# Delta-rule attention and an MLP in one kernel: whole-array first units, blocked weights, and a new static order

## The chip, the cores and the metric

The kernel runs on one core of a Trainium2 chip. A core has five engines with queues of their own: TensorE (PE, matrix products, written to the PSUM banks), VectorE (DVE), ScalarE (ACT), GpSimd (POOL) and SyncE (SP, which mostly issues DMAs). The metric is the device time of one execution in microseconds (us); the runs of one kernel on one chip are summed up by their median.

## The reference

For 4 batches and 8 heads, a recurrence runs over 768 tokens with a 48 x 48 state per head, and the result, 3072 tokens of 384 numbers, goes through an MLP:

```
k_n = k / (norm(k) + 1e-6)
for t in range(768):
    y[t]  = q[t] @ state
    v_old = state.T @ k_n[t]
    state = state + beta[t] * outer(k_n[t], v[t] - v_old)
x = y, heads side by side          # 3072 x 384
h = x @ w_in                       # 384 x 2048
out = gelu_tanh(h) @ w_out         # 2048 x 384
```

Inputs and output are float32; inside, the kernel works in bfloat16 with float32 sums.

## The kernel before

**Chunks and units.** The 768 tokens are cut into 12 chunks of 64. Within a chunk the recurrence is solved with matrices: the 64 x 64 triangular system of the chunk is inverted, and one state is carried from chunk to chunk. A chunk has two units (two batches each, 8 heads, so 128 partitions hold two batches by 64 tokens): 24 units u, 12 chunks c. For each unit `prep(u)` normalises k (`kn`), multiplies by beta (`kb`), casts q (`qb`), transposes the three (`T` on TensorE into `kT`; from unit 10 on by a DMA), builds two Gram matrices (`G2`, `G`) that VectorE copies under triangular masks into `ln` and `wp`, and inverts the triangle in five rounds of a Newton-like iteration. A round has a product `A` on TensorE, an addition `rt` (in rounds 4 and 5 the narrower `rl`) on VectorE, a product `B` on TensorE and a copy of `B` out of PSUM to be the next round's left operand `xi`.

**Two forms of a product.** For units 2 and up the left operand stands block-diagonally in `bd` (two 64 x 64 blocks in a 128 x 128 matrix), so that a product is 8 matmuls of the whole array (`L577`); the copies of `B` go into `bd` in two halves on ScalarE or VectorE (`bde`), or by way of `xi` and GpSimd (`bdc`), and the first round's `bd` is written by two GpSimd selects (`X1`). For units 0 and 1 (`u < TILED`) the operand stays in `xi` as two 64 x 64 halves, and a product is 16 matmuls on quarters of the array (`L580`); one copy on ScalarE carries `B` into `xi`.

**State and MLP.** `chain(c)` then reads the state (`K`, `R`, `Q`), applies the inverse (`U`, copied to `us`), updates the state (`S`, `Sn`) and makes the output (`O`, copied to `xo`), which is transposed (`X`, `xT`). `mlp(c)` runs 48 up matmuls (3 to a block of 128 columns of w_in, `L715`), four gelu instructions on ScalarE (`L720`) and 32 down matmuls (`L728`), evicts two 128 x 384 results (`Z`) and stores them.

**What sets the order.** No engine's order is written by hand. Every operation is added to a list with its engine or engines, an estimated duration, what it reads and writes, and a key. `Flow.schedule` plays the list through on estimated times, takes at each engine the ready operation of the lowest key (with offsets from a table `KEYS` and some thresholds), and so fixes five queues; `Flow.emit` writes them out with semaphore waits. On the chip each queue then runs strictly in that order. For TensorE the planner counts instructions in blocks of 256 (`BLOCK`) and lets the next block come `REFILL` us after the last one was entered. `FILL` dummy matmuls on a zero tile `wz` (`L426`) are put in where the planner finds TensorE with nothing ready; what is left of them runs last.

**Weights.** `weights()` casts w_in and w_out to bfloat16 in DMAs that GpSimd issues: `W1` of [128, 3, 2048] and `W2` of [128, 16, 384], two DMAs each, so rows of 1024 and of 384 columns. They wait until k and q of chunks 1 and 2 have landed. GpSimd issues them in the midst of the preparation of units 2 to 5.

**Tables and norms.** `norms(c)` makes the reciprocal norms of k: a square, a reduce, a root (on ScalarE for the first three chunks), eps and a reciprocal.

Of the kernel before, what the change touches and what calls it, by code (L numbers as in the profile page):

```python
# [24 lines left out]
class Flow:  # L25
# [5 lines left out]
    SLACK = 3.316  # L31
    DMA_LAT = 2.6
    DMA_AHEAD = 4.0
    BLOCK, REFILL = 256, 4.2
    STALL_SLACK = 0.316
    YIELD = 0.524
    KEYS = {"A": (-7.71, -5.16), "B": (-8.97, -24.42), "G": (-2.84, -18.0), "G2": (-29.12, -32.55), "K": (-9.35, 7.5),
            "O": (-7.72, 20.33), "On": (-12.86, -26.48), "Q": (-2.61, 7.53), "R": (-5.21, 3.94), "S": (2.29, 5.4),
            "Sn": (1.11, -13.13), "T": (1.64, -15.61), "U": (-6.61, 14.58), "Un": (11.48, -26.2), "X": (-18.72, -0.83),
            "X1": (-10.44, 4.23), "Z": (-11.93, -59.74), "bdc": (-1.39, -1.66), "bde": (-0.39, -30.53), "bdz": (5.03, 48.53),  # L40
            "down": (14.54, 27.08), "eps": (6.96, -24.93), "gelu": (0.92, 27.76), "inv": (-28.92, 24.92), "kT": (12.35, -2.18),
            "kb": (-6.15, -0.06), "kn": (28.23, 13.15), "ladj": (-11.45, 74.91), "ln": (7.96, -17.35), "loadk": (3.9, -10.38),
            "loadq": (4.06, -4.84), "loadv": (5.61, -10.9), "out": (10.45, -36.55), "pow": (-0.57, 2.88), "qb": (4.0, 12.65),
            "rt": (-17.56, -11.96), "sq": (-16.33, 39.05), "sum": (29.93, -44.43), "tabG": (-22.77, 16.06),
            "tri": (16.56, -21.66), "turn": (0.89, -16.45), "turnx": (-22.16, -15.64), "up": (1.24, -3.93), "w1": (-6.75, 17.06),
            "w2": (30.51, 0.26), "wp": (7.96, -30.95), "xT": (-16.66, -39.38), "xi": (1.34, -6.31)}
    PEN = 8.000
    HOLD = 0.219
    SOON = 0.3
# [41 lines left out]
    def schedule(self):  # L91
# [22 lines left out]
        count, refilled = 0, 0.0  # L114
        self.stalled = 0.0
# [7 lines left out]

        def run_pe(o, t):
            d = o.dur + (self.SWITCH if o.mode != mode else 0.0)
# [4 lines left out]
            while n >= left:  # L130
# [5 lines left out]
                ref, left = x + self.REFILL, self.BLOCK  # L136
# [38 lines left out]
        while done < len(self.ops):  # L175
            for e in ENGINES:
                while free[e] <= t + 1e-9:
                    o = choose(e)
# [118 lines left out]
def bass_deltanet__then__act_gelu_tanh_kernel(  # L297
# [13 lines left out]
    NU = 2 * NC  # L311
    DIRECT = lambda u: (2, 3, 4, 5) if u < 8 else (2, 4)
    GROUPS = [[c] for c in range(NC)]
    FILL = 60
    TILED = 2
    TURN, TURNX = 10, 5

    F = Flow()
    A = F.add
# [475 lines left out]
```

## Time and profile before

| | |
|---|---|
| median of 3 runs | 282.13 us (281.83 to 283.87) |
| the profiled execution's own time | 285.42 us |
| its span, from the first to the last instruction | 283.7 us |
| TensorE busy | 264.1 us, 93% |
| VectorE, ScalarE, GpSimd busy | 67%, 63%, 52% |
| mean granted TensorE clock | 0.976 |
| first up matmul of the MLP, last down matmul ended | 50.75 us, 279.96 us |

How to read a profile: a row of a timeline has start, duration, engine, line and operation, what it writes and reads, shapes and count, and in brackets the idle time of the engine before it with what ended it. "issue" there means that the engine waited for nothing that the profile shows. PEld is TensorE's weight load, which overlaps the matmuls. Matmuls are pipelined, so that a row's duration holds some latency, and the distance from one start to the next is the time that it takes from the ones behind it. In the slices of the page the span is cut in 40 parts of 7.09 us; a digit is the busy share in tenths, and PEclk the granted clock in tenths of full speed. q1 is the queue of SyncE's DMAs, q0 that of GpSimd's, and q8 carries the engines' own code. Each run's time is a little longer than its span.

### The profile page before, as it was taken

Reading aid. Unit: us, or ns where it says so; the run is one execution under the profiler, and the core shown is the slowest. Engines: PE = TensorE matmul, PEld = TensorE weight load, DVE = VectorE, ACT = ScalarE, POOL = GpSimd, SP = SyncE. Lnnn points to the kernel's source line nnn. Section 1 sums busy time; section 2 is a strip of 40 time slices with the busy share of each in tenths; the row PEclk is TensorE's granted clock in tenths of the full one; section 3 lists DMA queues with packets and bytes.
Section 4 is the critical chain, followed back from the end, with each engine's and each line's share of the span. In section 5 each row is a group of like instructions: output and inputs, shape, how many; then the busy total and the mean of one; then the engine's idle time right before and its main releaser. Section 6 shows DMA issues by size and latency. Waiting matters only on the chain.

```text
span 283.7 us, 12884 instructions
## 1 busy us (share of the span) xinstructions
PE 264.1 (93%) x5849; PEld 201.6 (71%) x5860; DVE 189.0 (67%) x291; ACT 178.7 (63%) x274; POOL 147.3 (52%) x217
## 2 busy tenths in 40 slices
PE   4789487999999999899998999999999999999997
PEld 1356367787778777687777777778777787878663
DVE  7797556876977987787998857496576777430000
ACT  5715245699767775576785683786766775756421
POOL 4468810257899299787699895442443431200000
PEclk9999777799999999999999999999999999999999
DMA  7999999960698923999991392760696210300133
GB/s 122 164 163 175 196 187 161 156 110 2 125 154 144 166 36 65 159 174 160 173 124 31 70 145 45 146 111 2 116 140 116 58 30 5 58 2 2 30 83 83
DMA packets 109237, 29.72 MB, mean 105 GB/s; under 512 B 103296, under 2 KB 108416, under 8 KB 109184
## 3 DMA queue, kind: packets, MB, share of 16 engines
q1 hardware_dynamic: 104848, 25.47, 57.7%
q0 software_dynamic: 2880, 3.15, 7.0%
q8 instruction: 46, 0.75, 1.1%
q10 hardware_dynamic: 1456, 0.30, 0.5%
q14 instruction: 7, 0.06, 0.1%
HBM read 20.64 MB, written 4.72 MB: 89 GB/s over the span
## 4 chain that ended last, share of the span: by engine, by line
PE 83%; DVE 6%; ACT 5%; issue 4%; POOL 1%; POOLq 0%
PE ps L728 22%; PE ps L715 22%; PE ps L577 17%; PE ps L426 4%; PE ps L626 3%; PE ps L648 3%; PE ps L671 3%; PE ps L520 2%; ACT bd L369 2%; PE ps L580 2%; PE ps L536 2%; PE ps L544 2%; ACT gT L720 1%; PE ps L657 1%; DVE rt L587 1%
## 5 line engine op out<-in xcount | busy, mean ns | idle before, releaser
L715 PE MATMUL ps<-xT,W 128*128 128x256 bf16 x576 | 85.6, 274 | 0.6 <-ACT gT L720 0.3
L728 PE MATMUL ps<-W,gT 128*128 128x384 bf16 x384 | 74.5, 326 | 0.1
L369 ACT ACTIVATE bd<-ps 64x512 bf16<-64x512 f32 x93 | 54.8, 589 | 18.6 <-PE ps L577 17.2
L587 DVE TENSOR_TENSOR rt<-ps,two 128x512 bf16<-128x512 f32 x72 | 48.8, 686 | 17.6 <-PE ps L577 16.5
L720 ACT ACTIVATE gT<-ps 128x1024 bf16<-128x1024 f32 x48 | 48.8, 1022 | 15.6 <-PE ps L715 15.3
L369 ACT ACTIVATE xi<-ps 128x512 bf16<-128x512 f32 x57 | 33.6, 596 | 31.0 <-PE ps L577 17.7
L715 PEld LDWEIGHTS ps<-xT,W 128*128 128x128 bf16 x576 | 47.6, 98 | 7.7 <-ACT gT L720 0.8
L566 POOL TENSOR_SCALAR_AFFINE_SELECT bd<-ln 64x512 bf16<-64x512 bf16 x44 | 28.9, 656 | 41.2 <-DVE ln L548 37.6
L728 PEld LDWEIGHTS ps<-W,gT 128*128 128x128 bf16 x384 | 34.8, 98 | 17.8 <-issue 0.3
L570 POOL COPY bd<-xi 64x256 f32<-64x256 f32 x64 | 25.4, 397 | 32.5 <-ACT xi L369 24.9
L587 DVE TENSOR_TENSOR rl<-ps,two 128x384 bf16<-128x384 f32 (+1 forms) x48 | 23.1, 485 | 15.4 <-PE ps L577 12.2
L552 DVE CAST_PREDICATED wp<-mup,ps 128x1024 bf16<-128x1024 uint16 x24 | 29.2, 1218 | 2.4 <-PE ps L536 2.1
L488 POOL TENSOR_TENSOR nrm<-nrm,half 128x16 f32<-128x16 f32 x9 | 26.2, 2908 | 3.1 <-DVE nrm L485 2.7
L577 PE MATMUL ps<-wp,bd 128*128 128x64 bf16 (+1 forms) x528 | 25.6, 190 | 1.2 <-issue 0.8
L577 PE MATMUL ps<-rt,bd 128*128 128x64 bf16 x528 | 26.5, 195 | 0.2 <-DVE rt L587 0.2
L512 POOL TENSOR_TENSOR tok<-tok,bsb 128x384 bf16<-128x384 bf16 x23 | 18.7, 830 | 12.9 <-PE ps L657 6.4
L577 PEld LDWEIGHTS ps<-rt,bd 128*128 128x128 bf16 x528 | 22.6, 99 | 3.3 <-DVE rt L587 0.3
L577 PEld LDWEIGHTS ps<-wp,bd 128*128 128x128 bf16 x528 | 21.1, 99 | 4.6 <-issue 1.0
L369 ACT ACTIVATE ob<-ps 128x384 f32<-128x384 f32 x23 | 11.3, 490 | 16.0 <-PE ps L728 15.8
L426 PE MATMUL ps<-wz 128*128 128x512 bf16 x49 | 15.6, 445 | 5.0 <-POOL wz L375 4.0
L510 POOL TENSOR_TENSOR tok<-kraw,nrm 128x384 bf16<-128x384 f32 x22 | 17.9, 831 | 3.0 <-DVE nrm L492 2.8
L548 DVE CAST_PREDICATED ln<-mlo,ps 128x512 bf16<-128x512 uint16 x24 | 16.3, 684 | 4.6 <-PE ps L544 4.5
(90 smaller groups left out, 349.2 us busy)
## 6 DMA issues: line engine op xcount, KB each, us to landing
qraw<-in_q_dram SPq DMA_DIRECT2D x24, 192.0 KB, 5.3
vraw<-in_v_dram SPq DMA_DIRECT2D x24, 192.0 KB, 5.4
out_dram<-ob SPq DMA_DIRECT2D x48, 96.0 KB, 2.7
kraw<-in_k_dram SPq DMA_DIRECT2D x22, 192.0 KB, 5.3
W<-in_moe_w_in_dram POOLq DMA_DIRECT2D x2, 768.0 KB, 10.3
W<-in_moe_w_out_dram POOLq DMA_DIRECT2D x2, 768.0 KB, 13.4
kT<-tok SPq DMA_TRANSPOSE x14, 4.6
kraw<-in_k_dram ACTq DMA_DIRECT2D x2, 96.0 KB, 3.2
```

What stands on the lines that cost most here:

```text
L369: return e.activation(out, in_, ACT.Copy) if e is nc.scalar else e.tensor_copy(out, in_)
L426: ins = e.matmul(P(name)[:, :], wz[:, 0:128], wz[:, 0:512])
L488: e.tensor_tensor(nr[:, 1, hx], nr[:, 0, hx], half[:, hx], ALU.pow), {"act": 0.22, "pool": 1.65 * wd},
L512: A(POOL, z + "kb", lambda e, P: e.tensor_tensor(kb, kn, bcol, ALU.mult), tt, reads=[n("tok0"), *BS], writes=[n("tok1")], key=u)
L552: A("dve", z + "wp", lambda e, P: e.copy_predicated(wp[s][:, :, :], mup[:, :].bitcast(U16).unsqueeze(1).to_broadcast([128, H, 2 * C]), P(p ...
L566: A("pool", z + "X1", lambda e, P, src=src, dst=dst: e.affine_select(out=dst, in_=src, compare_op=ALU.not_equal, fill=1.0, base=0, pattern ...
L570: A("pool", z + "bdc", lambda e, P, src=src, dst=dst: e.tensor_copy(dst.bitcast(F32), src.bitcast(F32)), 0.42, reads=[n("xi")], writes=[w( ...
L577: ins = e.matmul(P(name)[:, C * h + lo:C * h + C], bd[m][:, h, :], rhs[:, h, lo:C])
L587: A("dve", z + "rt", lambda e, P, i=i, lo=lo, r_=r_: e.tensor_tensor(r_[:, :, lo:C], P(ps(f"A{i}")).rearrange("p (h t) -> p h t", h=H)[:, ...
L715: ins = e.matmul(P(ph)[:, w * f:w * f + w].rearrange("p (x t) -> p x t", x=2), W1[:, j, 128 * (i + f):128 * (i + f) + 128], x_[:, :, j, :] ...
L720: A("act", z + "gelu", lambda e, P, i=i, ph=ph: e.activation(g_[:, i:i + nf, 0:w], P(ph).rearrange("p (f t) -> p f t", f=nf), ACT.Gelu_app ...
L728: ins = e.matmul(P(po)[:, 0:DM], g_[:, f, 128 * b:128 * b + 128], W2[:, f, :], start=(f == 0), stop=(f == FC - 1))
```

## The change

Four things change together.

- **First units:** `TILED` is 0, so units 0 and 1 go the block-diagonal way too (8 whole-array matmuls to a product, selects on GpSimd for the first round, half copies after that).
- **Weights:** `W1` is kept as [128, 8, 3, 256] and `W2` as [128, 2, 16, 192]. Six DMAs fill `W1` and four `W2`, with rows of 256 and 192 columns. The up matmul's weights stay 128 columns side by side; the down matmul reads its 384 columns as two pieces of 192.
- **Engines:** the zero tile `wz` is written by VectorE first of all; q's cast for units 0 and 1 goes to ScalarE or VectorE instead of GpSimd or VectorE; one of the two first kT copies may go to ScalarE; the squares of chunks 1 and 2 go to ScalarE, and all norms of chunk 1 get a very early key.
- **Order:** the planner gets a TensorE clock (half speed after a window of 3.4 us that was not busy enough), a slower code refill while weights load, other thresholds and keys, and 110 dummies instead of 60. The first up of a chunk's MLP now also waits, in the plan, for the downs of three chunks earlier that read the same gelu buffer. All five queues come out in another order.

In the order for TensorE that results, 77 dummies stand ahead of the first up (48 before), 20 more between it and the last down (3 before) and 13 behind that (9 before); units 2 and 3 begin their rounds just ahead of the first up, where before they had done about half of them.

The core of the diff:

```diff
-    BLOCK, REFILL = 256, 4.2
+    BLOCK, REFILL = 256, 3.9
...
+    WINDOW = 3.413
+    PHASE = 1.094
+    SLOW = 2.4
+    LOW, HIGH = 0.6, 0.93
...
+        def roll(t):
+            nonlocal cold, edge, active
+            while edge <= t:
+                share = active / self.WINDOW
+                cold = share < (self.HIGH if cold else self.LOW)
+                edge, active = edge + self.WINDOW, 0.0
...
-            d = o.dur + (self.SWITCH if o.mode != mode else 0.0)
+            d = (o.dur + (self.SWITCH if o.mode != mode else 0.0)) * (2.0 if cold else 1.0)
...
-                ref, left = x + self.REFILL, self.BLOCK
+                ref, left = x + self.REFILL + (self.SLOW if crowd[0] < x < crowd[1] else 0.0), self.BLOCK
...
-    FILL = 60
-    TILED = 2
+    FILL = 110
+    TILED = 0
...
+    SQACT, EARLY, QBACT, KTACT = 3, -140, 1, 1
...
-        W1 = sb("W1", [128, J, FF])
-        W2 = sb("W2", [128, FC, DM])
+        W1 = sb("W1", [128, FC // 2, J, 256])
+        W2 = sb("W2", [128, 2, FC, DM // 2])
...
-            A("pool", "0wz", lambda e, P: e.memset(wz[:, :], 0.0), 0.5, writes=["wz"], key=-30)
+            A("dve", "1wz", lambda e, P: e.memset(wz[:, :], 0.0), 0.2, writes=["wz"], key=-200)
...
-            for i in range(2):
-                f0 = FF // 2 * i
-                A("pool", "w1", lambda e, P, f0=f0: e.dma_start(W1[:, :, f0:f0 + FF // 2], w1v[:, :, f0:f0 + FF // 2]), 4.7,
+            for i, j in [(i, j) for i in range(2) for j in range(J)]:
+                f0, b0 = FF // 2 * i, FC // 4 * i
+                A("pool", "w1", lambda e, P, j=j, f0=f0, b0=b0: e.dma_start(
+                    W1[:, b0:b0 + FC // 4, j, :], w1v[:, j, f0:f0 + FF // 2].rearrange("p (b f) -> p b f", f=256)), 4.7 / J, mm=0.35,
...
-            for i in range(2):
-                n0 = FC // 2 * i
-                A("pool", "w2", lambda e, P, n0=n0: e.dma_start(W2[:, n0:n0 + FC // 2, :], w2v[:, n0:n0 + FC // 2, :]), 4.7,
+            for i, y in [(i, y) for i in range(2) for y in range(2)]:
+                n0, e0 = FC // 2 * i, DM // 2 * y
+                A("pool", "w2", lambda e, P, n0=n0, y=y, e0=e0: e.dma_start(W2[:, y, n0:n0 + FC // 2, :], w2v[:, n0:n0 + FC // 2, e0:e0 + DM // 2]), 2.35, mm=0.5,
...
-                key = 2 * c + x
-                A("dve" if c == 0 else ("act", "pool"), z + "sq", lambda e, P, sqx=sqx, kk=kk: e.activation(sqx, kk, ACT.Square) if e is nc.scalar else
+                key = 2 * c + x if c != 1 or not EARLY else EARLY
+                z = z if c != 1 or not EARLY else "1"
+                A("dve" if c == 0 else "act" if c < SQACT else ("act", "pool"), z + "sq", lambda e, P, sqx=sqx, kk=kk: e.activation(sqx, kk, ACT.Square) if e is nc.scalar else
...
-            A(POOL, z + "qb", lambda e, P: e.tensor_copy(qb, qr), {"pool": 0.5, "dve": 0.4}, reads=[f"qraw{r}"], writes=[n("tok2")], key=u + 0.01)
+            A((("act", "dve") if QBACT else POOL) if u < 2 else "pool", z + "qb", lambda e, P: copy(e, qb, qr), {"pool": 0.5, "dve": 0.4, "act": 0.55}, reads=[f"qraw{r}"], writes=[n("tok2")], key=u + 0.01)
...
-                      **(dict(alloc=(ph, 2)) if f == 0 else dict(accum=[ph])))
+                      **(dict(alloc=(ph, 2), writes=[f"{gn}s{i}"]) if f == 0 else dict(accum=[ph])))
...
-                            ins = e.matmul(P(po)[:, 0:DM], g_[:, f, 128 * b:128 * b + 128], W2[:, f, :], start=(f == 0), stop=(f == FC - 1))
+                            ins = e.matmul(P(po)[:, 0:DM].rearrange("p (y e) -> p y e", y=2), g_[:, f, 128 * b:128 * b + 128], W2[:, :, f, :], start=(f == 0), stop=(f == FC - 1))
```

## The prediction, made before the changed kernel was run

> **What bounds the kernel now.** I read the page first, for the engine shares and the slices, then TensorE's timeline between 26 and 62 us, then the chain of work that ended last near the end, and last the groups by shape. From the page:
>
> ```profile
> PE 264.1 (93%) x5849; PEld 201.6 (71%) x5860; DVE 189.0 (67%) x291; ACT 178.7 (63%) x274; POOL 147.3 (52%) x217
> ...
> PE   4789487999999999899998999999999999999997
> ...
> PEclk9999777799999999999999999999999999999999
> ...
> q1 hardware_dynamic: 104848, 25.47, 57.7%
> q0 software_dynamic: 2880, 3.15, 7.0%
> q8 instruction: 46, 0.75, 1.1%
> ```
>
> TensorE is the bound from slice nine (57 us) on; only in the first eight slices does it idle or run at a reduced clock. So the case splits in a head, where latency rules, and a body, where every TensorE instruction counts. The head, in TensorE's timeline:
>
> ```profile
> 34.54 0.50 PE L580 MATMUL ps<-wp,xi 64*64 64x32 bf16 x11 [3.12 <-issue]
> ...
> 38.13 0.92 PE L648 MATMUL ps<-rs,xi 64*64 64x48 bf16 x27
> ...
> 41.25 0.59 PE L671 MATMUL ps<-us,wp 64*64 64x48 bf16 x27 [0.98 <-issue]
> ...
> 47.57 0.27 PE L626 MATMUL ps<-st,kT 48*64 48x48 bf16 x10 [1.37 <-issue]
> ...
> 50.75 0.82 PE L715 MATMUL ps<-xT,W 128*128 128x256 bf16 x3
> ```
>
> Three waits for "issue" stand inside runs of equal matmuls. Counted in the built program (two instructions to a matmul, one to a separate wait), they lie 257 and 255 instructions apart, and q8 moved 46 pieces of 16 KB for 11,825 instructions: TensorE waited for its own code, at 34.54, 41.25 and 47.57, so one block of 256 took 6.7 and 6.3 us to come while the weights were loading. Late in the run the next such waits end a block of 3.7 us (111.98 to 115.70). A rule of the Trainium skill (Runtime: NRT & Kernel Launch, Instruction fetch mechanics) is that crossing a block costs little and is mostly hidden; these three rows speak against it, and by it the sum below would be 2.5 us lower.
>
> The first MLP matmul starts at 50.75. From the chain near the end:
>
> ```profile
> 256.45 3.93 PE ps L715 x36
> ...
> 264.96 14.95 PE ps L728 x92
> ...
> 279.96 1.89 PE ps L426 x8
> ```
>
> An up matmul takes 3.93/36 = 0.109 us, a down 14.95/92 = 0.1625, and the last down ends at 279.96, 3.7 before the span's end (an eviction and a store).
>
> **TensorE's sum, part by part.** In the same way the chain and the timeline give 0.22 us for one block-diagonal product of 8 (three of them, x24, in 0.67), 0.37 for one of 16 quarter-array matmuls (20.36 to 20.73), 0.056 for a transpose, 0.216 for a dummy (1.89 for 8, with its latency), and 0.1 for each change between quarter-array and whole-array instructions (four downs behind such a change stand with 0.76 in the chain, else with 0.65). Multiplied with the order of instructions that each program gives TensorE:
> - Real work (all but dummies): before 239.9, after 233.4. Of the 6.5, 20 products of units 0 and 1 at 0.37 minus 0.23 give 2.9, and 194 changes of mode become 156, 38 by 0.1 = 3.7.
> - Before the first up: before 21.1, after 13.3, since units 2 and 3 no longer invert ahead of it. From there to the last down: before 218.8 and 3 dummies (0.65), after 220.1 and 20 dummies (4.3). The last 13 dummies (2.8) lie beside the final store (3.7) and cost nothing.
> - Against the trace: 279.96 - 50.75 = 229.2, so the body loses 9.8 that the sum does not hold: about 1.3 to the half clock until 53, 8.5 to short waits.
>
> W2 is now read in two pieces of 192 columns. The up matmul already reads its moving operand in two pieces of 128 and takes 0.109 us for 256 columns, so I add nothing.
>
> **The head.** The cast of q leaves VectorE for ScalarE (0.98), one kT copy too (0.91), but chunk 1's norms move between the masks of ln and wp: reduce 0.93, eps 0.4, reciprocal 0.25, and ln of unit 1 waits behind a reduce that waits for ScalarE's square. So wp of units 0 and 1 is done where it was, near 19.5, and the inversion starts as before (18.5). A round has four steps: product 0.42 until its consumer starts, rt 0.69, product 0.42, copy 0.6 to 0.69. VectorE bears two rt and two of the four half copies, 1.37 + 1.38 = 2.75, where ScalarE's xi copies left it 1.37 before. Two rounds at 2.8, one with the reduce (0.93) at 3.7, two with the shorter rl at 2.5 end at about 32.5; the xi copy, and U starts at 33.5. Before, U started at 38.13, 3.1 of that behind the code stall. That stall goes because a block-diagonal round issues half the matmuls; what is late next is again code: in the new order blocks end between O and S and just ahead of units 2 and 3's first products. With a block requested at 31.5 and 6.5 us each, TensorE gets them at 38 and 44.5. Without a stall, the copies of kT, us, two wp, two ln and the state on VectorE (0.95 + 0.96 + 2.4 + 1.4 + 0.95 ahead of kT of unit 4) let the first up start at 42. So 42 and 44.5 bound it.
>
> **Ten weight DMAs.** GpSimd's two rows are these:
>
> ```profile
> L471 POOL DMA_DIRECT2D W<-in_moe_w_out_dram x2 | 1.8, 911 | 0.0
> L467 POOL DMA_DIRECT2D W<-in_moe_w_in_dram x2 | 1.8, 878 | 0.0
> ```
>
> 1024 rows cost what 384 do, but both move the same bytes: an issue costs 0.9 per DMA, or in proportion to bytes 0.3 (w1, a third) and 0.45 (w2, half). Six w1 take 1.8 to 5.3 us against 1.75. Behind them on GpSimd stand the casts, kn and kb of units 2 and 3 (1.0, 1.65, 1.62), which start after the four selects (about 18.2): unit 2's tokens are ready at 23.8 to 27. TensorE's order holds unit 2's transpose ahead of unit 1's second product of round two, due at 23.9, so all behind it waits 0 to 3 us. The two rows cannot part the ends; I take the middle, 0.6, which makes 1.4 late, and 1 of it reaches the first up: 45.5. On cost by DMA the Trainium skill (DMA: Bandwidth & Descriptors, Anatomy of one DMA) says that many descriptors can be emitted before the added cost shows, and lists the fixed part apart; it speaks for the upper end, and with it the sum would be about 2 higher.
>
> Bytes on the queues: q1's packets of 243 B mean took 0.577 x 16 x 283.7 / 104848 = 25 ns, q0's of 1094 B 110 ns, in both 10 B per ns, so 512 and 384 B rows cost no more by byte. With twice the rows against q1's, and q1 served in between, I expect w2 to end near 50 where it ended near 44; the first downs are due past 52. That cover is 2 to 4 us.
>
> **Sum.** First up 45.5, work 220.1, dummies 4.3, short waits 8.5, half clock after the idle head 2.0 (as before, since TensorE does about 3.5 us of work between 34 and 44.5), tail 3.7: a span of 284.1. The profiled execution had a span of 283.7 and took 285.42, the runs' median is 282.13: 285.8 x 282.13/285.42 = **282.5 us, no change**. The first up comes 5 us sooner, and the work that stood ahead of it, with 17 more dummies, is paid behind it.
>
> **Rivals.**
> - Faster: the smaller packets let code through in the 3.7 us of the late blocks, and dummies keep the clock up. First up 42, no half clock: 278.6, which is **277.1 us**. For it: 77 dummies ahead of the first up, where the old order has 48. Against it: 2 KB packets (until 31) and 768 B packets (after) made code equally late.
> - Slower, decided by the price of one issue on GpSimd: from 0.6 up it holds unit 2's transpose, and with it TensorE's queue. At 0.9 the first up is at 47.5, span 286.1, **284.5 us**; with the weights later by the same 3 us and the first downs waiting on them up to 2 more, 286.5.
> - The body loses more: the new order's 20 dummies mark places where its plan found nothing ready, and if TensorE's short waits there rise by half again (8.5 to 13) and the second half of W2 is late by 1: 289.6, **288 us**. Against it: VectorE and ScalarE are busy 67% and 63%, and their work hardly changes.
> - It doesn't do what it says: the changes of mode cost nothing because they lie in waits. Then 3.7 come back, **286.2 us**; it counts with the third case.
>
> **How the numbers follow.** About 1% (2.8 us) is what a measurement of this kernel can tell from no change. Forecast 0.37, faster rival 0.28, slower rival 0.22 (half of it beyond 1%), body rival 0.13. Faster by over 1%: 0.28; within: 0.37 + 0.11 = 0.48; slower: 0.11 + 0.13 = 0.24. The range 277 to 288 leaves out the outer parts of the first and last rivals, some 0.15.
>
> **What would show it.** First up at 45 to 46 and waits for "issue" of 1 to 2.5 us at S and ahead of it; GpSimd's W issues between 0.3 and 0.9 us; unit 2's first transpose at 24 to 27; the clock under full between 36 and 49; VectorE's bd copies 8 before U. A first up at 42 or below, or a body with under 6 us of waits, makes it faster and this wrong; W2 landing after 54 makes it slower.

## The result and the profile after

The changed kernel takes **296.2 us** (median of 4 runs, 296.16 to 296.98) where the kernel before takes 282.95 (281.83 to 283.87): a ratio of **1.046** (95% interval 1.042 to 1.050). This ratio and those below leave out runs more than 1.5% above the fastest of their kernel. The forecast was 282.5, the range 277 to 288: it was wrong. The profiled execution of the changed kernel took 296.16 with a span of 294.3.

The page of the changed kernel, its lines that answer to those shown of before (busy time and instructions; the slices, now 7.36 us each; the DMA queues):

```profile
PE 273.6 (93%) x5750; PEld 204.1 (69%) x5750; DVE 196.2 (67%) x310; ACT 176.8 (60%) x269; POOL 145.6 (49%) x219
...
PE   8995955999899999899998999899999999999998
...
PEclk9997995999999999999999999999999999999999
...
q1 hardware_dynamic: 104848, 25.47, 54.8%
q0 software_dynamic: 7328, 3.15, 8.4%
q8 instruction: 45, 0.74, 1.1%
```

TensorE has 110 matmuls fewer (PEld has 5860 and 5750; the trace of before lacks 11 records of PE) and is busy 9.5 us longer: busy time also holds the dummies, 110 instead of 60, and the stretches at half clock. In the row of slices, from slice nine to the last but one, four stand below nine tenths, where before had two.

TensorE's timeline of the changed kernel around the head (start, duration, what it does, and in brackets the idle time ahead of it):

```profile
25.89 1.46 PE L545 MATMUL ps<-ident,tok 128*128 128x128 bf16 x12 [2.95 <-POOL tok L537]
...
36.55 0.62 PE L673 MATMUL ps<-rs,xi 64*64 64x48 bf16 x28
...
41.48 0.44 PE L682 MATMUL ps<-us,tok 64*64 64x48 bf16 x32 [2.50 <-DVE ln L573]
...
48.59 0.32 PE L561 MATMUL ps<-kT 48*64 48x128 bf16 x3 [2.76 <-issue]
...
49.69 2.11 PE L740 MATMUL ps<-xT,W 128*128 128x256 bf16 x9
```

Unit 2's transpose waits 2.95 us for GpSimd's tokens, U starts at 36.55, and two waits for code follow, at S and in the Gram matrices ahead of the first up. The one at 41.48 is put down to VectorE's `ln`; counted in the built program, it stands at instruction 194 of its block of 256, as the one at 48.59 (195) does, and in no_body_dummies below, whose queues are the same up to the first up, the wait there is put down to "issue". The block between them took 7.1 us. The first up starts at 49.69.

The end, from the chain of work that ended last:

```profile
283.35 7.15 PE ps L753 x44
290.50 2.81 PE ps L449 x13
```

The last down ends at 290.50 and the span 3.8 later, as before. So the time went here: first up 50.75 to 49.69 (1.1 sooner), first up to last down 229.2 to 240.8 (**11.6 longer**), the rest unchanged.

Where in the body? Windows of the two kernels (stretch, its length, busy time of PE with its instructions, then PEld, DVE, ACT, POOL, clock, DMA), before:

```profile
110.00:140.00 30.00, 29.20 (x805) 22.85 (x805) 24.43 (x38) 19.09 (x28) 23.98 (x37) 1.00 0.98 160
...
165.00:200.00 35.00, 34.45 (x858) 26.44 (x857) 24.01 (x35) 24.61 (x39) 17.77 (x33) 1.00 0.45 86
```

and after:

```profile
110.00:140.00 30.00, 27.56 (x758) 21.77 (x756) 24.57 (x39) 18.27 (x28) 22.62 (x34) 1.00 0.80 135
...
165.00:200.00 35.00, 32.67 (x801) 25.01 (x801) 28.70 (x43) 22.25 (x36) 18.62 (x37) 1.00 0.50 84
```

Over the body TensorE's idle time is 7.7 us (4.0 before), 3.1 of it in waits for code (1.4 before). At full clock it idles 2.4 and 2.3 us in these two stretches, where it idled 0.8 and 0.6, and part of its busy time there is dummies. One such place, in TensorE's timeline of the changed kernel:

```profile
187.72 0.36 PE L602 MATMUL ps<-wp,bd 128*128 128x32 bf16 x8
188.70 0.41 PE L602 MATMUL ps<-wp,bd 128*128 128x64 bf16 x8 [0.62 <-DVE wp L577]
188.95 0.40 PE L602 MATMUL ps<-rt,bd 128*128 128x64 bf16 x8
189.18 0.72 PE L602 MATMUL ps<-rl,bd 128*128 128x64 bf16 x16
190.03 0.39 PE L449 MATMUL ps<-wz 128*128 128x512 bf16 x1
190.26 0.40 PE L602 MATMUL ps<-rt,bd 128*128 128x64 bf16 x8
190.49 1.03 PE L449 MATMUL ps<-wz 128*128 128x512 bf16 x4
```

Only products of inversions stand here, each behind a VectorE step of 0.7 to 1.2 us, and no up or down matmul is beside them: dummies fill what they can.

### The profile page after: what moved, and what is told of

It is laid out like the page before. It is cut to its first block, busy times and chain, and to the rows that moved or that the text cites. A ratio compares the mean times of both kernels' runs of the same rounds, so it can differ in the third digit from the quotient of the medians.

```text
span 294.3 us, 12706 instructions
## 1 busy us (share of the span) xinstructions
PE 273.6 (93%) x5750; PEld 204.1 (69%) x5750; DVE 196.2 (67%) x310; ACT 176.8 (60%) x269; POOL 145.6 (49%) x219
## 3 DMA queue, kind: packets, MB, share of 16 engines
q0 software_dynamic: 7328, 3.15, 8.4%
HBM read 20.64 MB, written 4.72 MB: 86 GB/s over the span
## 4 chain that ended last, share of the span: by engine, by line
PE 77%; DVE 10%; POOL 4%; issue 3%; ACT 2%; DMA 2%; SPq 1%; POOLq 0%
PE ps L753 21%; PE ps L740 21%; PE ps L602 17%; PE ps L449 4%; DVE wp L577 2%; PE ps L545 2%; PE ps L561 2%; PE ps L651 2%; PE ps L673 2%; PE ps L696 2%; DVE rt L612 2%; DMA braw<-in_beta_dram 2%; PE ps L569 2%; POOL W L490 2%; POOL bd L591 1%
## 5 line engine op out<-in xcount | busy, mean ns | idle before, releaser
L740 PE MATMUL ps<-xT,W 128*128 128x256 bf16 x576 | 83.9, 276 | 0.0
L740 PEld LDWEIGHTS ps<-xT,W 128*128 128x128 bf16 x576 | 49.5, 99 | 8.4 <-ACT gT L745 0.3
L591 POOL TENSOR_SCALAR_AFFINE_SELECT bd<-ln 64x512 bf16<-64x512 bf16 x48 | 31.4, 655 | 41.1 <-DVE ln L573 33.3
L595 POOL COPY bd<-xi 64x256 f32<-64x256 f32 x64 | 25.2, 395 | 34.9 <-ACT xi L392 26.9
L392 ACT ACTIVATE xi<-ps 128x512 bf16<-128x512 f32 x46 | 27.1, 596 | 18.0 <-PE ps L602 17.6
L577 DVE CAST_PREDICATED wp<-mup,ps 128x1024 bf16<-128x1024 uint16 x24 | 29.1, 1214 | 5.7 <-PE ps L561 5.6
L449 PE MATMUL ps<-wz 128*128 128x512 bf16 x110 | 31.1, 401 | 1.6 <-DVE wz L398 1.3
L602 PE MATMUL ps<-rt,bd 128*128 128x64 bf16 x576 | 29.3, 195 | 2.1 <-DVE rt L612 0.9
L392 DVE CAST bd<-ps 64x512 bf16<-64x512 f32 x34 | 23.1, 688 | 10.2 <-PE ps L602 9.6
L602 PEld LDWEIGHTS ps<-rt,bd 128*128 128x128 bf16 x576 | 24.7, 99 | 6.5 <-DVE rt L612 3.1
L602 PE MATMUL ps<-wp,bd 128*128 128x64 bf16 (+1 forms) x576 | 27.5, 190 | 1.4 <-DVE wp L577 0.6
L537 POOL TENSOR_TENSOR tok<-tok,bsb 128x384 bf16<-128x384 bf16 x23 | 19.0, 843 | 17.8 <-PE ps L682 11.6
L602 PEld LDWEIGHTS ps<-wp,bd 128*128 128x128 bf16 x576 | 23.0, 99 | 5.6 <-DVE wp L577 1.4
```

Of the source, the lines that this page charges most:

```text
L392: return e.activation(out, in_, ACT.Copy) if e is nc.scalar else e.tensor_copy(out, in_)
L449: ins = e.matmul(P(name)[:, :], wz[:, 0:128], wz[:, 0:512])
L537: A(POOL, z + "kb", lambda e, P: e.tensor_tensor(kb, kn, bcol, ALU.mult), tt, reads=[n("tok0"), *BS], writes=[n("tok1")], key=u)
L577: A("dve", z + "wp", lambda e, P: e.copy_predicated(wp[s][:, :, :], mup[:, :].bitcast(U16).unsqueeze(1).to_broadcast([128, H, 2 * C]), P(p ...
L591: A("pool", z + "X1", lambda e, P, src=src, dst=dst: e.affine_select(out=dst, in_=src, compare_op=ALU.not_equal, fill=1.0, base=0, pattern ...
L595: A("pool", z + "bdc", lambda e, P, src=src, dst=dst: e.tensor_copy(dst.bitcast(F32), src.bitcast(F32)), 0.42, reads=[n("xi")], writes=[w( ...
```

## The experiments

The body's loss below is worked out as in the prediction: first up to last down, less TensorE's work in that order of instructions, less its dummies. "Work" is what the prediction's times per instruction make of each program. First up and body come from the one profiled execution of each run, which need not lie at the median.

| kernel | median | ratio (95%) | first up | body | work, dummies | loss |
|---|---|---|---|---|---|---|
| before | 282.95 | | 50.75 | 229.2 | 218.8, 0.65 | 9.8 |
| changed | 296.2 | 1.046 (1.042 to 1.050) | 49.69 | 240.8 | 220.1, 4.3 | 16.4 |
| old_weights | 292.4 | 1.032 (1.025 to 1.039) | 44.56 | 240.7 | 220.0, 4.3 | 16.4 |
| no_body_dummies | 297.2 | 1.052 (1.045 to 1.059) | 47.86 | 242.4 | 219.8, 0 | 22.6 |
| old_planner | 293.2 | 1.033 (1.029 to 1.038) | 45.43 | 241.9 | 221.2, 0 | 20.7 |
| blocked_in_old_order | 286.7 | 1.012 (1.006 to 1.017) | 51.74 | 228.0 | 218.7, 0.65 | 8.7 |
| replanned_ten | 284.3 | 0.999 (0.994 to 1.005) | 43.00 | 234.6 | 220.3, 0.9 | 13.4 |
| part_weights | 289.5 | 1.021 (1.016 to 1.025) | 42.01 | 241.8 | 220.0, 4.3 | 17.4 |
| replanned_four | 282.8 | 0.987 (0.981 to 0.992) | 44.62 | 228.8 | 219.6, 0.9 | 8.4 |
| replanned_four_again | 282.6 | 0.984 (0.980 to 0.988) | 52.70 | 226.3 | 219.6, 0.9 | 5.8 |
| replanned_four_b | 287.2 | | 44.95 | 231.7 | 220.7, 1.3 | 9.7 |
| w1_behind | 279.0 | 0.981 (0.978 to 0.985) | 43.84 | 228.0 | 219.6, 0.9 | 7.6 |
| replanned_before | 281.1 | 0.988 (0.984 to 0.992) | 47.76 | 228.5 | 220.4, 0.6 | 7.5 |

Each ratio is against the kernel before on the same chip (medians there 282.95 to 284.6).

### The weights part undone: old_weights

The queues of the changed kernel as they are, but W1 and W2 in the old layout and six of the ten issues taken out:

```diff
-        W1 = sb("W1", [128, FC // 2, J, 256])
-        W2 = sb("W2", [128, 2, FC, DM // 2])
+        W1 = sb("W1", [128, J, FF])
+        W2 = sb("W2", [128, FC, DM])
...
         F.schedule()
...
+        for o in F.queues["pool"]:
+            if o.name in ("w1", "w2"):
+                if o.dma in first:
+                    gone.append(o)
+                first.setdefault(o.dma, o)
+        drop(gone)
```

> All five queues of the changed kernel, with the weights alone put back: four DMAs with rows of 1024 and 384 columns where six and four stood. Theory A (the price of ten issues on GpSimd sets the head): GpSimd is free for unit 2's tokens 3.0 us sooner, TensorE's wait of 2.95 us at unit 2's transpose goes, U starts near 33.5 instead of 36.55, the first up comes at 46 to 47 instead of 49.69, and the run is 3 us shorter, near 293. Theory B (code blocks hold the first up, whatever GpSimd does): the wait moves to the block boundaries, the first up stays at 48.5 or later, and the run is within 1 us of the changed kernel's 296.2. Theory C (the cost lies in the body of the new order) expects 290 or more either way.

The first up comes 5.1 us sooner, at 44.56 (1.4 below the range of theory A), the body is the same to 0.1, and the median is 3.8 us shorter:

```profile
23.48 0.84 PE L545 MATMUL ps<-ident,tok 128*128 128x128 bf16 x12 [0.32 <-POOL tok L537]
...
44.56 1.86 PE L740 MATMUL ps<-xT,W 128*128 128x256 bf16 x7
```

The issues of the changed kernel on GpSimd, and then of this one:

```profile
17.75 4.72 POOL L490 DMA_DIRECT2D W<-in_moe_w_in_dram  x6
...
27.46 3.58 POOL L495 DMA_DIRECT2D W<-in_moe_w_out_dram  x4
```

```profile
18.30 1.75 POOL L490 DMA_DIRECT2D W<-in_moe_w_in_dram  x2
...
25.06 1.82 POOL L495 DMA_DIRECT2D W<-in_moe_w_out_dram  x2
```

An issue costs 0.79 and 0.89 with a third and a half of the bytes, 0.88 and 0.91 with all of them: the price goes mostly with the number of DMAs. Here unit 2's transpose is at 23.48 instead of 25.89, and runs in 0.84 instead of 1.46, because in the changed kernel's profiled execution the granted clock was halved from 25.6 to 29.1. So 2.4 us on GpSimd became 3.9 at U (32.67 against 36.55). That half clock does not come each time: in no_body_dummies, with the same ten issues and the same order up to the first up, TensorE waits 2.04 us for the tokens and keeps the full clock until 38.4, U is at 34.55 and the first up at 47.86. So 1.8 of the 5.1 us belong to that one execution. Both code waits are still there (at 37.25 and 43.81): they move with the work and do not pin the first up to a time, so theory B falls.

### The dummies of the body taken out: no_body_dummies

```diff
+        q = F.queues["pe"]
+        at = [i for i, o in enumerate(q) if o.name == "up"][0]
+        end = [i for i, o in enumerate(q) if o.name == "down"][-1]
+        gone = [o for i, o in enumerate(q) if at < i < end and o.name == "fill"]
+        drop(gone)
```

> The changed kernel without the 20 dummy matmuls that stand between the first up and the last down; the order of all else is kept. If TensorE is the bound where they stand, they cost what they take: 20 x 0.216 = 4.3 us, so about 292. If they lie in waits that would be there anyway, the run changes by less than 1 us, and the waits ahead of the instructions behind them grow by the same amount. Without them every later block of 256 instructions ends up to 40 instructions later in the program, so the waits for code should fall on other instructions, still 194 or 195 beyond a multiple of 256.

The head of this kernel, whose queues are those of the changed kernel up to the first up:

```profile
25.36 0.84 PE L545 MATMUL ps<-ident,tok 128*128 128x128 bf16 x12 [2.04 <-POOL tok L537]
...
47.86 2.11 PE L740 MATMUL ps<-xT,W 128*128 128x256 bf16 x9
```

Nothing is gained: the loss grows from 16.4 by more than the 4.3 that the dummies took, since the clock falls to half once more (3.4 us at 168.13), and the time cannot be told from the changed kernel's (the intervals of the two ratios overlap). The dummies lay in waits that are there without them.

### The old planner with the new parts: old_planner

All four parts but the order: `KEYS`, thresholds, `FILL` and the planner's model of before.

```diff
-    SLACK = 4.906
+    SLACK = 3.316
...
-    FILL = 110
+    FILL = 60
```

> All parts of the change (block-diagonal first units, ten weight DMAs, zero tile and casts on other engines, early norms) with the planner's constants, keys and 60 dummies of the kernel before, so the queues come out in yet another order, with 235.3 us of real TensorE work. Theory C (the new order costs the time): near the kernel before, 281 to 286. Theory A (the ten issues and the parts cost it): 290 or more.

The body loses 20.7 without a dummy in it, and the median is in the range of theory A. So it is not the new table in itself: the table of before, on the new parts, makes a body just as slow. That left two readings: the block-diagonal first units push work behind the first up that cannot be covered there, or neither table suits the program that it is used on.

### The blocked weights in the old order: blocked_in_old_order

The kernel before, each weight DMA replaced in its place in GpSimd's queue by its share of the ten.

```diff
+        for o in F.queues["pool"]:
+            if o.name in ("w1", "w2"):
+                fns = parts[o.dma]
+                for j, fn in enumerate(fns[:-1]):
...
+                    queue.append(c)
...
+                o.fn = fns[-1]
+            queue.append(o)
```

> The kernel before with its five queues, each of its four weight DMAs replaced on the spot by its share of the ten. GpSimd is held 3.0 us longer ahead of the tokens of units 2 and 3, and 1.8 us more at w_out. Theory A: the transposes of units 2 and 3 (26.97 and 28.48) come 3 us later, and with them all behind; the run is 2 to 4 us longer, 285 to 287. Theory B: the code that TensorE waits for until 34.54 covers it, and the run is within 1 us of the kernel before. If smaller packets let code through, the waits of 3.12, 0.98 and 1.37 us for code shrink and the run is shorter than before.

The runs are 1.2% slower, the time of theory A. The profiled execution, the quickest of the four, has a span of 283.5 where the profiled one of before has 283.7, so it does not show where the 1.2% goes. It shows how most of the price hides, in the way of theory B: the issues take 4.72 and 3.59 as in the changed kernel, but unit 2's transpose was at 26.9 in the old order anyway and is at 26.82 here, and what comes after is held by code. Smaller packets (7328 in the weights' queue instead of 2880) did not hasten the code:

```profile
33.63 0.36 PE L580 MATMUL ps<-wp,xi 64*64 64x32 bf16 x11 [2.41 <-issue]
40.63 0.63 PE L671 MATMUL ps<-us,wp 64*64 64x48 bf16 x27 [1.70 <-issue]
...
47.85 0.36 PE L626 MATMUL ps<-st,kT 48*64 48x48 bf16 x10 [2.45 <-issue]
```

The blocks took 7.0 and 7.2 us, where 6.7 and 6.3 were read in the kernel before.

### Another order for the same work: replanned_ten

Every operation of the changed kernel stays; the table `KEYS` and six constants are others, and the planner is told 0.88 us for each weight issue. The table was found by random changes to the old one, each kept or dropped by when the program's own planner expects the list to end.

```diff
-    KEYS = {"A": (-11.97, 5.4), "B": (-7.1, -32.27), "G": (-6.11, -7.96), "G2": (-26.18, -29.74), "K": (-13.93, -13.54),
...
+    KEYS = {"A": (-33.03, -18.05), "B": (-50.34, -251.94), "G": (-18.24, -138.16), "G2": (-47.66, -139.64), "K": (-28.33, -99.75),
...
-                    W1[:, b0:b0 + FC // 4, j, :], w1v[:, j, f0:f0 + FF // 2].rearrange("p (b f) -> p b f", f=256)), 4.7 / J, mm=0.35,
+                    W1[:, b0:b0 + FC // 4, j, :], w1v[:, j, f0:f0 + FF // 2].rearrange("p (b f) -> p b f", f=256)), 4.7 / J, mm=0.88,
```

> The changed kernel with another table of ordering keys and six other ordering constants: every instruction of the block-diagonal units and of the ten weight DMAs stays, only the order in which the queues hold them is another. Its TensorE work ahead of the first up is 12.2 us (changed kernel 13.2), from there to the last down 220.3 (220.0), with 4 dummies there (0.9 us, changed kernel 20 with 4.3). Theory D (the body's loss lies in the order that was written out, which lets inversion rounds of TensorE, VectorE and ScalarE stand with nothing beside them, and not in the block-diagonal work itself): the body from first up to last down falls from 240.8 to 229-233, its loss from 16.4 to 9-11; the head stays at 48-51, since the ten issues and the code blocks are as they were; the span is 282-288, the time 281-288, ratio to the kernel before 1.00-1.02. Theory E (the work that the block-diagonal units push behind the first up, 10 us more on VectorE, cannot be covered there in any order): the body stays at 238-242, the time at 293-298, ratio 1.035-1.05.

12 us of the 13 that the change had cost are gone, with nearly the same work on each side of the first up. Theory E falls: from the first up to the last down VectorE is busy 158.6 us here and 158.3 in the changed kernel (151.9 before), and it can be covered. Theory D was right on the cause and wrong on the split: the body fell by 6.2, not by 8 to 12, and the first up by 6.7, where none was expected. This order has unit 2's transposes near the end of chunk 0's inversions. The tokens are late there too:

```profile
32.84 0.84 PE L546 MATMUL ps<-ident,tok 128*128 128x128 bf16 x12 [3.12 <-POOL tok L538]
```

But U starts at 34.73 (36.55 in the changed kernel), between U and the first up TensorE waits for code 1.0 us instead of 5.3, and the next wait for code, 1.9 us at 47.03, falls behind the first up.

The body's loss can be split by an estimate from the traces: waits for code, and half of the time that the clock was halved. The changed kernel's 16.4 has 3.1 and 1.6, which leaves 11.7; replanned_ten's 13.4 has 4.3 and 2.6, which leaves 6.5; the 9.8 of before has 1.4 and 1.1, which leaves 7.3. So what the other order takes away is the part that is neither code nor clock, and the dummies with it.

Where the inversions starved in the changed kernel, between 165 and 200, TensorE is now full (windows of replanned_ten):

```profile
110.00:140.00 30.00, 27.53 (x757) 21.99 (x754) 21.57 (x32) 18.30 (x28) 22.31 (x32) 0.94 1.20 159
140.00:165.00 25.00, 25.00 (x617) 20.69 (x615) 21.08 (x36) 19.74 (x32) 21.87 (x30) 1.00 0.57 104
165.00:200.00 35.00, 35.00 (x896) 27.73 (x892) 25.04 (x37) 23.52 (x36) 17.84 (x32) 1.00 0.59 89
```

Most of what is left of the loss above before's lies at 47.03 and between 110 and 140: two waits for code there (1.1 and 1.4 us) and a window at half clock behind them.

### A part of the weights: part_weights

```diff
-                    W1[:, b0:b0 + FC // 4, j, :], w1v[:, j, f0:f0 + FF // 2].rearrange("p (b f) -> p b f", f=256)), 4.7 / J, mm=0.35,
+                    W1[:, b0, j, :], w1v[:, j, f0:f0 + 256]), 4.7 / J, mm=0.35,
...
-                A("pool", "w2", lambda e, P, n0=n0, y=y, e0=e0: e.dma_start(W2[:, y, n0:n0 + FC // 2, :], w2v[:, n0:n0 + FC // 2, e0:e0 + DM // 2]), 2.35, mm=0.5,
+                A("pool", "w2", lambda e, P, n0=n0, y=y, e0=e0: e.dma_start(W2[:, y, n0, :], w2v[:, n0, e0:e0 + DM // 2]), 2.35, mm=0.5,
```

> The changed kernel, same order, same ten DMAs, but each moves only its first block: 256 of 1024 columns for w1 (128 rows of 512 B instead of 512), one of eight row groups for w2 (128 rows of 384 B instead of 1024). Leaves out: three quarters of the first and seven eighths of the second weight matrix, every matmul reads the one loaded block of its half. It asks two things. Price of an issue on GpSimd: theory A (by DMA) has 0.75-0.95 us each as before, unit 2's first transpose at 25-26.5; theory F (by rows or bytes) has 0.3-0.5 each, the transpose at 23-24.5. Late code: theory G (the weights' traffic on the DMA engines delays the code blocks) has the waits for issue at about 41.5 and 48.6 go or shrink below 0.5, the blocks between take 4-4.7 us instead of 6.7 and 7.1, first up at 45-46.5; theory H (the code is late for another reason, such as GpSimd's issuing or the loads of q, k and v) has the waits at 2-3 us as before and the first up at 48.5-50. The body is 239-242 in all of them, so the time is 291-293 under A with G, 295-297 under A with H.

On late code the answer is clear: with a fifth of the weights' bytes (0.59 of 3.15 MB) the second wait is gone, of the first at most 0.4 us is left, and the first up comes at 42.01.

```profile
37.00 0.60 PE L682 MATMUL ps<-us,tok 64*64 64x48 bf16 x32 [0.44 <-DVE wp L577]
...
41.20 0.40 PE L561 MATMUL ps<-kT 48*64 48x128 bf16 x16
41.53 0.64 PE L602 MATMUL ps<-wp,bd 128*128 128x64 bf16 x16
42.01 0.49 PE L740 MATMUL ps<-xT,W 128*128 128x256 bf16 x3
```

The weights' traffic makes the code late. (This run cuts the packets as well as the bytes, 1440 instead of 7328; that it is the bytes is argued from blocked_in_old_order, where 2.5 times the packets for the same bytes made a block 0.3 to 0.9 us longer.) The time is below what was expected under that theory, because the first up came 3 us sooner than 45. On the price of an issue neither theory holds whole:

```profile
18.08 3.43 POOL L490 DMA_DIRECT2D W<-in_moe_w_in_dram  x6
...
26.51 2.18 POOL L495 DMA_DIRECT2D W<-in_moe_w_out_dram  x4
```

0.57 and 0.55 each, and the transpose of unit 2 at 24.94, between the two forecasts: over half a microsecond stays when three quarters of the rows, or seven eighths, are gone, and 0.2 to 0.35 goes with them.

### A good order with four weight DMAs: replanned_four

The changed kernel with the weights of before (two DMAs each, old layout) and a table found for it in the same way.

> Block-diagonal first units and the planner of the changed kernel, the weights in the old layout by four DMAs, and a table of ordering keys made for this program. Work ahead of the first up 13.5 us, from there 219.6 and 4 dummies. Theories D and A (issues cost GpSimd 0.8 to 0.95 each whatever they move, and that cost the changed kernel 5 us ahead of the first up): first up at 43.5-46, body 228-232, span 276-281, time 275-281, ratio 0.975-0.995: faster than both kernels. Theory E: first up 43.5-46, body 238-242, time 290-294. A third theory, that four DMAs gain nothing once the order is good, would have it within 1 us of replanned_ten.

Body and loss come out as theories A and D had it, the loss below before's. old_weights has the same four DMAs and the same operations, and its body is 240.7 instead of 228.8. The planner also chose other engines for some copies here: in the body VectorE is busy 153.4 us (159.1 in old_weights) and ScalarE 158.3 (154.6), so the gain over old_weights is that of the new order and of this shift together. But the runs fell in two kinds, 278.84 and 280.64 beside 285.04 and 287.13, and 0.987 is the ratio of the first two. It was run again:

> The same kernel as replanned_four once more, with more rounds: there two of four runs took 278.8 and 280.6 us and two 285 and 287, so what it gains over the kernel before is not settled. If the good runs are its normal time and the others chance (the half clock and the late code fall differently from run to run): ratio 0.980-0.992, most runs at 278-282. If the others are as normal: runs spread from 278 to 287, the median at 282-284, ratio 0.99-1.00, and the gain over the kernel before is within what can be told from no change.

278.87, 278.97 and 279.89 beside 285.38, 286.12 and 286.69: both are normal for this kernel, whose six runs have a mean of 282.7, where the kernel before has 283.8 beside them. This time the profile took one of the longer ones. ScalarE in the short kind, then in the long kind:

```profile
22.06 0.84 ACT L508 ACTIVATE sq<-kraw 128x768 f32<-128x768 f32 x1 [0.16 <-DMA kraw<-in_k_dram]
```

```profile
31.46 0.84 ACT L508 ACTIVATE sq<-kraw 128x768 f32<-128x768 f32 x1 [9.35 <-DMA kraw<-in_k_dram]
```

The square of chunk 2's k stands in ScalarE's queue ahead of the copies that the inversions need, and in the long kind its k lands 9 us late; the first up is at 52.70 instead of 44.62. That k comes in two DMAs. In the long kind the first was issued at 15.09 and the second, which the square waits for longest, at 17.20, beside weights issued at 17.39; in the short kind the second was issued at 15.89 and the weights at 17.86. Between 19 and 20 us the weights' packets have begun in the long kind, and SyncE's queue moves 150 packets; in the short kind they have not, and it moves 612. The DMA queues of the long kind between 22 and 28 us:

```profile
q0 software_dynamic: 532, 1.06, 94.5%
q1 hardware_dynamic: 534, 0.10, 15.7%
```

The weights' queue and SyncE's took turns, packet by packet, 2 KB against 192 B: what is left of k's load when the first weights start comes at a tenth of the rate. That is what the Trainium skill states (DMA: Bandwidth & Descriptors, Queues, rings and completion order: each DMA engine goes round its queues one packet at a time), and the counts agree as far as they go: a packet there holds several descriptors, and the trace's records here are single rows.

A second table found for the same program:

> As replanned_four with another table of ordering keys found in the same way: work ahead of the first up 13.6 us, from there 220.7 with 160 changes of mode (replanned_four 219.6, 148) and 6 dummies. Theory D (an order with work beside each inversion loses about what the kernel before loses, whatever the table): first up 43.5-46, body 229-234, time 277-284, ratio 0.98-1.00. If the gain of replanned_four came from this one table by luck: body 236-242, time 287-294.

Its profiled execution has a body of 231.7 with a loss of 9.7, as theory D expects, so the good body was not one table's luck; its time was in the range only in two of six runs (282.2 to 291.3, median 287.2, where the kernel before has 283.7), and two tables for one program are 4.6 us apart in the median. No profile of the longer ones was taken, so whether the same race makes them was not settled.

### The first weights behind the tokens: w1_behind

replanned_four, with the two DMAs of w_in moved in GpSimd's queue behind the `kb` of unit 3:

```diff
+        at = [i for i, o in enumerate(rest) if o.name.endswith("kb")][2]
+        F.queues["pool"] = rest[:at + 1] + first + rest[at + 1:]
```

> replanned_four with one edit in GpSimd's queue: the two DMAs of the first weight matrix stand behind the last kb of unit 3 instead of ahead of kn of unit 2, so they are issued at about 21.5-22.5 instead of 17.9. In the slow one of replanned_four's two kinds of run ScalarE's square of chunk 2 waited 9.4 us for the k load that was issued at 15.1, and the chain of the inversions stood behind it for 8.2 us; the weights' packets had begun before that load's had ended, and beside them q1 moves one packet for each packet of q0 (534 and 532 between 22 and 28 us), that is a tenth of the bytes. Theory J (that race between the k load and the first weights makes the two kinds of run): all runs at 277-281.5, none over 283; first up at 43-46, ratio 0.978-0.988. Theory K (the two kinds come from somewhere else): again runs at 285-287 beside runs at 279. The weights now come 4 us later; if the first up waits for them, it is at 46-48 and the time 281-283 in all runs.

Five runs from 278.38 to 279.77, none longer: theory J. In the profile the issues start at 22.59 and the square runs at 22.22 without a wait for its load. **This kernel beats both**: 0.981 of before. Its page:

```profile
PE   8999867999999999899999999999999999999999
...
PEclk9999977999999999999999999999999999999999
```

Its chain ends with 22 dummies that were left over:

```profile
271.88 4.91 PE ps L450 x22
```

They outlast the final store: the span ends 5.2 us after the last down, where in the kernel before and in replanned_before it ends 3.7 after it. By this estimate some 1.5 us could be had by fewer dummies; no run shows it.

### A search for an order alone: replanned_before

The kernel before with a table and constants found in the same way; nothing else is changed.

> The kernel before with another table of ordering keys and six other ordering constants, found in the same way as those of replanned_four; all its work stays (32 of 64 columns per product in units 0 and 1, four weight DMAs). Work ahead of the first up 19.1 (kernel before 21.1), from there 220.4 (218.8), 3 dummies. It asks whether what replanned_four gains over the kernel before comes from the block-diagonal first units or from the search for an order alone. If from the units (6 us less work for TensorE): ratio 0.99-1.01. If from the search: 0.975-0.99.

It gains 1.2%, in the range of "from the search", whose upper end of 0.99 lies inside the interval. So of the 1.9% of w1_behind the larger part is not owed to the block-diagonal units. w1_behind is some 0.7% quicker still, with intervals (0.978 to 0.985, 0.984 to 0.992) that hardly touch. The bodies of the two are alike (228.0 and 228.5); the first up of w1_behind is 3.9 us sooner, and its leftover dummies take 1.5 back. That the block-diagonal units are worth the 0.7% is not shown: the two kernels also have different tables, and only one of them had its weight DMAs moved.

## Why the prediction was wrong

The sum was 45.5 + 220.1 + 4.3 + 10.5 + 3.7 = 284.1; the trace has 49.7 + 220.1 + 4.3 + 16.4 + 3.8 = 294.3.

- **What bounds the kernel, and the sum of work: right.** TensorE's work per stretch holds: the body contains the 220.1 and the 20 dummies, and the work taken from ahead of the first up is paid behind it. Two more pieces of 192 columns in the down matmul cost nothing (44 in 7.15 is 0.1625, as before).
- **"Short waits 8.5", carried over from before: the step that failed most, 5.9 us.** The body's loss is 16.4, not 10.5: half clock 1.6 of it (2.0 forecast), the rest 14.8. The term was taken as a property of the kernel's machinery; it is a property of the order that was written out. replanned_ten shows it: the same operations in another order, 3.0 less loss and 3.4 less in dummies, although it met more late code (without code and half clock the loss is 6.5 instead of 11.7, by the estimate above). Of the 16.4, 7.7 is idle time in the profile; the rest, but for the half clock, lies inside what counts as busy, and what it is made of stays open. The prediction's third rival named the mechanism ("dummies mark places where its plan found nothing ready"), gave it 0.13, argued it down with the engines' mean busy shares, and put it at 13. Busy shares of 67% and 63% say nothing on whether a queue has independent work at the moment that a chain needs cover. no_body_dummies settles that the dummies were sign and not cause.
- **An issue at 0.6, "1 of it reaches the first up": 4.2 us too small.** The bounds of 0.3 and 0.9 held, the middle was the wrong pick: it is 0.79 and 0.89. The prediction weighed a statement of the Trainium skill for the upper end (DMA: Bandwidth & Descriptors, Anatomy of one DMA: many descriptors can be emitted before the added cost shows), and the upper end was nearer; but 0.2 to 0.35 of an issue did go with the rows or bytes (part_weights). Beyond the price, the step missed what can follow a late transpose: in the profiled execution the clock was halved from 25.6 to 29.1, so that 2.4 us late became 3.9 at U and 5.1 at the first up (old_weights); in no_body_dummies it was not, and the first up is at 47.86. The second rival had the mechanism of the price, with the first up at 47.5.
- **The head without that price: right.** U was forecast at 33.5 and is at 32.67 in old_weights; the first up bounded by code at 44.5 and there at 44.56; the waits of 1 to 2.5 at S and in the Gram matrices are 2.2 and 2.5 there (2.5 and 2.8 in the changed kernel).
- **Late code and the small packets: right, with the cause left open there.** Smaller packets do not let code through (7.0 to 7.2 us a block). What neither the prediction nor its faster rival said is that the weights' traffic is the cause: with a fifth of the bytes and of the packets the first up is at 42.01, the time at which the prediction put the unstalled head. How the traffic delays the code is not shown. (The three waits of before lie 255 and 257 instructions apart, in this order.) The rule that crossing a block is mostly hidden (the Trainium skill, Runtime: NRT & Kernel Launch, Instruction fetch mechanics) fits that run's head and fails beside a heavy queue.
- **W2 late: hidden, as forecast.** By the packets of q0 it ended at 49.4, where about 50 was expected.
- **The last 3.5 us: the scaling.** The profiled execution of before was one of its longer runs, so the sum was scaled down by 282.13/285.42, 3.3 us; the changed kernel's profiled run lies at its median. A factor from one execution did not carry to this kernel.

## What to carry to other kernels

In a kernel whose queues are written out by a planner, a new order is a change of its own: before crediting a part with a gain, go through the new queue and see what stands beside each dependent chain, and take the loss of the old order for the old order's alone. A table of keys tuned to one program need not be tuned to its neighbour; re-tune for each variant before they are compared, with more than one table each, and judge a transformation only then. Cutting a DMA into more pieces costs its issuing engine for every piece, and matters most where that engine's next work feeds the critical chain.

## What the runs showed of the hardware that had not been expected

- Between SyncE's queue and GpSimd's the DMA engines took turns by packet, nearly one for one, with packets of 2 KB beside 192 B (532 and 534) and roughly so with 512 B (1359 and 1574). With rows of 512 B instead of 2 KB, in the changed kernel between 22 and 28 us, q1 moves 0.30 MB where it moved 0.10 in replanned_four's long kind:

```profile
q0 software_dynamic: 1359, 0.68, 85.2%
q1 hardware_dynamic: 1574, 0.30, 39.6%
```

  In these two traces, then, the smaller the weights' packets, the less a load beside them is slowed, which is a reason for small packets that the changed kernel's order did not use.
- A 9 us difference in a load's landing, and 7 in the kernel's time, went with 1.3 us in the issue of that load (15.89 or 17.20), beside weights issued at 17.86 or 17.39; with the weights issued at 22.59 all five runs were short. What moves the issue from run to run is not shown.
- The waits put down to "issue" of 0.9 us or more end at instruction 194 or 195 of a block of 256 (two to a matmul, one to a separate wait), in the traces of all kernels here, whatever stands there; why there is not shown.
